# Attention and two gated layers on one core: a home for the sums of squares, chunk two's start and the last statistics planned with the next part, layer 2's decoding spaced

## The chip, the cores and the metric

The kernel runs on one core of one Trainium2 chip. A core has a matrix engine (TensorE, PE in the profile, with weight loads shown apart as PEld), a vector engine (DVE), an activation engine (ACT), a general engine (GpSimd, POOL) and a synchronising engine (SP) that here issues the transfers. The metric is the device time of one execution in microseconds, lower is better. Times of the trace are counted from the first instruction of its span.

## The reference, cut to what matters

```python
def reference(q, k, v, moe, moe2):            # q, k, v: 4 batches, 8 heads, 576 tokens, 64
    scores = where(mask, q @ k.T / 8, -1e9)   # heads 0-3: the last 32 positions,
    a = softmax(scores) @ v                   # heads 4-7: every 32nd position
    x = a.transpose(0, 2, 1, 3).reshape(2304, 512)
    xn = x / sqrt(mean(x * x) + 1e-6) * rms_g
    y = (silu(xn @ w_gate) * (xn @ w_val)) @ w_out         # 512 -> 1536 -> 512
    h = y @ w_in2                                          # 512 -> 2048
    return softplus(h) @ w_out2                            # 2048 -> 512
```

## The kernel before, in words

Each fp32 product is made of three products of halves: a number is split into a high part and the rest, both stored in a reduced matmul type, and `mm3` multiplies high by high, low by high and high by low. So `ob` (normalised tokens), `win` and `wout` (weights), `gh`/`gl` (gated values) and `tb` all come in pairs: ACT makes the high part (L257, L313, L333, L724) and DVE or POOL subtracts it for the rest (L262 on DVE, L264 on POOL). The tokens are cut into chunks at `CUTS` 0, 512, 1024, 1536, 2048, 2304. Chunks 0 and 1 are **side one**, computed plainly; chunks 2 to 4 are **side two**, where sums of chunks (`combine`, `build`, tile `tb`) and of weights let seven products stand for eight (`quad`).

Weights arrive as 64-bit words. `decode` turns one 128x512 block into fp32: a transfer into `raw` (512 KB, L277), one ACT instruction (L278), three DVE instructions (L279, L281, L284), and a transfer of the result to `w_kept` in DRAM (L287), from where later passes fetch it. A step f of layer 1 has three such blocks (`prep1`: two for `win`, one for `wout`); side two decodes layer 2's blocks ahead of time (`early2`).

The order of every engine's instructions comes from a planner. `pr.add` records work for an engine with an estimated duration; each `pr.emit()` closes a **part**, in which the planner lays out the recorded work by these estimates. Work in `side = True` is a second PE stream that is fitted in between the first. On each engine a part's instructions all come after those of the part before. The parts that matter here:

- Part 1: attention of batches 0 and 1 (`attend`, tiles without a tag). Each output block is squared and added up by POOL into `ssq`, the **sums of squares of side one** (128x1024). In the gaps stand the statistics of chunk 0 (`stats(0)`: a PE product of `ssq` with ones L356, ACT's Ln L358 and Exp L359, three DVE instructions L360, L362, L363, then `norm`, which multiplies the tokens `xs` by the result), `direct(0)` (the split into `ob`), and the `half` products of layer 1's steps f=0 and 1. At the end the same for chunk 1 (`stats(1)`, `direct(1)`) and the first two `chain1` (silu L735, product L736, split).
- Part 2: `side_a(f)` for f = 0 to 9 (f below `DEALT`), mixed with the attention of batches 2 and 3, whose tiles have the tag b (`klb0`, `qlb0`, `ksb0`, `qsb0` hold keys and queries; the first are loaded at L425 and L427 and completed with fixed patterns by DVE L390 and POOL L394). At its end stand the statistics of chunks 3 and 4, the **last turn**.
- Part 3: `side_a(10)`, `side_a(11)`, then `combine` and `build` of side two, its layer 1 (12 steps with a `quad` each), then layer 2 over both sides with `prep2` for its weights. `out1` (L769) and `out2` (L787) add finished products to `xs`.

The pool `at` of part 1 also holds `ssq`; part 2's pool `at2` reuses the same memory for the b tiles.

Of the kernel before, what the change touches and what calls it, by code (L numbers as in the profile page):

```python
# [27 lines left out]
CH = 512  # L28
# [8 lines left out]
DEALT = 10  # L37
LT, LT2, LV, EB = 4, 4, 5, 5
WARM = 9
EXTRA = {"gv": 2, "gh": 3, "gl": 3}  # L40
START = 14
HOLD = (12, 14)
# [122 lines left out]
def attn_glu_softplus(  # L165
# [36 lines left out]
    class Ring:  # L202
        def __init__(self, tiles, name, first=0):
            self.t, self.name, self.first, self.k = tiles, name, first, -1

        def next(self):
            self.k += 1
            i = self.k % len(self.t)
            return self.t[i], (f"{self.name}{self.first + i}", 0, 1 << 20)

    tb, ssq = [], []

    def sview(lo, hi):
        return ssq[0][:, lo:hi] if hi <= TA else ssq_b[:, lo - TA:hi - TA]
# [11 lines left out]
    xs = const.tile([128, KD * NT], F32, name="xs")  # L226
    ssq_b = const.tile([128, TB], F32, name="ssq_b")
# [146 lines left out]
    def attention(at, tag, bs, nq2, nv, npt, nsq, s_banks, t_banks, v_banks):  # L374
# [10 lines left out]
        def fixed(i):  # L385
            def spread(eng, t, key, h, x0, n, w, c0):
                dst = t[64:128, h, x0:x0 + n * w].rearrange("p (n w) -> p n w", w=w)
# [216 lines left out]
    def steps(at, after, ring_):  # L604
# [29 lines left out]
        return out + [None, (turn, (), (3, 4))]  # L634
# [203 lines left out]
    def prep2(p, all4):  # L838
        i = ((W1N + p) % 2, 0)
        o = 3 * W1N + 4 * p  # L840
        prep_in(i, [(o, None), (o + 2, None)], True, all4, "DVE")
# [4 lines left out]
    with tc.manual_schedule():  # L846
# [25 lines left out]
        at_step(16, prepare, 0, (0, 1), HOLD[0])  # L872
        at_step(17, prepare, 1, (0,), HOLD[1])
        at_step(START, stats, 0, f_banks)
        at_step(START, direct, 0)
        for f, r_ in ((0, f_banks), (1, s_banks)):
            for row in (0, 1):
                at_step(18 + f, half, f, row, r_)
# [13 lines left out]
        with ExitStack() as c2:  # L892
            at = c2.enter_context(tc.tile_pool(name="at", bufs=1))
            ssq.append(at.tile([128, TA], F32, name="ssq"))
            attend(attention(at, "", (0, 1), 2, 3, 4, 2, s_banks, t_banks, v_banks), fill)
            stats(1, t_banks)
            direct(1)
            table("silu_and_others")
            for f in (0, 1):
                g[f, 0] = chain1(gates[f, 0], gates[f, 1])  # L900
# [3 lines left out]
        for key, dt in (("gv", F32), ("gh", F32R), ("gl", F32R)):  # L904
# [7 lines left out]
        def side_a(f, queue):  # L912

            if f:
# [14 lines left out]
        with ExitStack() as c2:  # L929
# [3 lines left out]
            x.fixed(0)  # L933
            queue = steps(x, {1: (2,)}, tv)
# [3 lines left out]
            step(queue, len(queue))  # L938
            pr.emit(start=0)
        o_banks.t = banks.t[4:6] + banks.t[2:4]  # L940
        wc = ctx.enter_context(tc.tile_pool(name="wc", bufs=1))
# [4 lines left out]
        for f in range(DEALT, W1N):  # L946
            side_a(f, [])
# [3 lines left out]
        o_banks.t = banks.t[4:]  # L951
        build(*SIDES[1], False)
        for f in range(W1N):
# [16 lines left out]
            early2(2 * f)  # L970
# [98 lines left out]
```

## Time and profile before

| what | value |
|---|---|
| median of 3 runs | 977.6 us (975.78 to 978.59) |
| the profiled execution, its own time | 977.51 us |
| its span, first to last instruction | 975.7 us |
| mean granted TensorE clock | 0.963 |
| PE busy | 908.3 us (93%) |
| DVE busy | 723.5 us (74%) |
| ACT busy | 489.0 us (50%) |
| POOL busy | 213.2 us (22%) |
| moved by DMA | 103.12 MB, 35.3% of the engines' span |

The profiled execution lies within the runs, 0.1 us under the median. Its time is 1.8 us longer than its span, which is what lies around the first and last instruction. PE is busy nearly throughout; a share is an average over parts with different limits, so the parts have to be looked at singly.

### The profile page before, as it was taken

How to read it: one execution, taken by the hardware profiler on the slowest of the kernel's cores; microseconds unless marked ns; L12 is line 12 of the kernel's file. 1: busy time of each engine (PE TensorE's matmuls, PEld its weight loads, DVE VectorE, ACT ScalarE, POOL GpSimd, SP SyncE). 2: the span in 40 equal slices, each digit the busy share in tenths (PEclk: the TensorE clock that was granted, in tenths of full speed). 3: DMA queues.
4: the chain of work that ended last, by engine and by line, in shares of the span. 5: the costliest groups of instructions: out<-in, count | busy, mean ns of one | idle time of the engine just before them, and what ended most of it. 6: DMA issues, size and time to landing. Idle time of an engine off the chain costs nothing.

```text
span 975.7 us, 14001 instructions
## 1 busy us (share of the span) xinstructions
PE 908.3 (93%) x5244; PEld 746.2 (76%) x5244; DVE 723.5 (74%) x1198; ACT 489.0 (50%) x917; POOL 213.2 (22%) x187
## 2 busy tenths in 40 slices
PE   6877799999959899999999997999998999999998
PEld 5755678777837678888888876888886888888886
DVE  7696768897359888597887888787779736666654
ACT  5565566555254546545354545744455464434431
POOL 2453102141144543243233353000004000000000
PEclk8777899999988999999999999999999999999999
DMA  9834766744005245233433403431110411111002
GB/s 205 197 123 119 214 208 181 229 127 150 1 23 179 85 136 184 75 125 120 135 109 98 154 9 108 162 104 59 54 57 20 152 44 44 25 41 44 22 1 108
DMA packets 42036, 103.12 MB, mean 106 GB/s; under 512 B 5040, under 2 KB 5744, under 8 KB 41968
## 3 DMA queue, kind: packets, MB, share of 16 engines
q1 hardware_dynamic: 41968, 102.23, 35.3%
q8 instruction: 41, 0.67, 0.3%
q14 instruction: 27, 0.22, 0.1%
HBM read 79.66 MB, written 22.54 MB: 105 GB/s over the span
## 4 chain that ended last, share of the span: by engine, by line
PE 77%; DVE 15%; issue 3%; ACT 3%; DMA 2%; POOL 0%; SPq 0%; DVEq 0%; ACTq 0%; POOLq 0%
PE bank L342 71%; PE bank L449 3%; DVE xs L262 2%; PE bank L530 2%; DVE w L262 2%; PE bank L506 1%; DVE xs L769 1%; DVE cvu L281 1%; DVE win L262 1%; DVE cvu L279 1%; DVE ob L262 1%; DVE tb L262 1%; DMA ql<-q_t 1%; DVE gvx L262 1%; DVE gv L688 1%
## 5 line engine op out<-in xcount | busy, mean ns | idle before, releaser
L342 PE MATMUL bank<-ob,win 128*128 128x512 f32 (+1 forms) x1560 | 343.6, 367 | 26.0 <-ACT win L313 11.4
L342 PEld LDWEIGHTS bank<-ob,win 128*128 128x128 f32 x1560 | 270.0, 193 | 78.4 <-ACT win L313 11.8
L342 PE MATMUL bank<-tb,win 128*128 128x512 f32 x672 | 172.7, 392 | 7.8 <-ACT gvx L684 3.6
L342 PEld LDWEIGHTS bank<-tb,win 128*128 128x128 f32 x672 | 124.1, 188 | 37.1 <-ACT gv L684 5.0
L787 DVE TENSOR_TENSOR xs<-bank,xs 128x512 f32<-128x512 f32 x126 | 86.7, 689 | 49.1 <-PE bank L342 48.6
L313 ACT ACTIVATE win<-w 128x512 fp32r<-128x512 f32 (+1 forms) x136 | 83.2, 615 | 77.8 <-DVE w L262 34.6
L262 DVE TENSOR_TENSOR win<-w,win 128x512 fp32r<-128x512 f32 x112 | 80.0, 715 | 22.3 <-ACT win L313 22.0
L342 PE MATMUL bank<-wout,ghx 128*128 128x512 f32 x304 | 94.0, 391 | 0.6 <-DVE xs L787 0.5
L342 PE MATMUL bank<-ghx,wout 128*128 128x512 f32 x224 | 86.0, 403 | 0.5 <-ACT ghx L724 0.5
L342 PE MATMUL bank<-gh,wout 128*128 128x512 f32 (+1 forms) x256 | 83.1, 362 | 3.0 <-DVE xs L769 2.9
L342 PE MATMUL bank<-wout,gh 128*128 128x512 f32 x272 | 84.0, 390 | 0.0
L769 DVE TENSOR_TENSOR xs<-bank,xs 128x512 f32<-128x512 f32 (+1 forms) x100 | 62.8, 631 | 24.9 <-PE bank L342 24.3
L262 DVE TENSOR_TENSOR w<-w 128x256 f32<-128x256 f32 x112 | 65.9, 588 | 1.3
L342 PEld LDWEIGHTS bank<-wout,ghx 128*128 128x128 f32 x304 | 56.6, 188 | 13.2 <-DVE xs L787 1.8
L342 PE MATMUL bank<-wout,glx 128*128 128x512 f32 x152 | 59.3, 390 | 0.3 <-DVE glx L262 0.3
L342 PEld LDWEIGHTS bank<-wout,gh 128*128 128x128 f32 x272 | 50.8, 188 | 10.8 <-DVE xs L787 0.4
L281 DVE SCALAR_TENSOR_TENSOR cvu<-raw,cvu 128x512 uint32<-128x512 uint32 x68 | 56.6, 833 | 1.3
L342 PEld LDWEIGHTS bank<-gh,wout 128*128 128x128 f32 x256 | 46.9, 194 | 11.4 <-DVE xs L769 4.3
L342 PE MATMUL bank<-wout,gl 128*128 128x512 f32 x136 | 52.9, 389 | 0.0
L342 PEld LDWEIGHTS bank<-ghx,wout 128*128 128x128 f32 x224 | 43.1, 192 | 10.3 <-ACT ghx L724 0.9
L688 DVE TENSOR_TENSOR gv<-bank,gv 128x512 f32<-128x512 f32 x48 | 33.0, 687 | 20.5 <-ACT gv L684 14.1
L342 PE MATMUL bank<-gl,wout 128*128 128x512 f32 (+1 forms) x128 | 46.2, 361 | 1.7 <-POOL gl L264 1.7
(157 smaller groups left out, 1357.5 us busy)
## 6 DMA issues: line engine op xcount, KB each, us to landing
raw<-w SPq DMA_DIRECT2D x68, 512.0 KB, 4.0
w<-w_kept SPq DMA_DIRECT2D x56, 256.0 KB, 2.7
w_kept<-w SPq DMA_DIRECT2D x24, 256.0 KB, 3.4
w_kept<-cvt SPq DMA_DIRECT2D x22, 256.0 KB, 2.9
w_kept<-cvtx SPq DMA_DIRECT2D x22, 256.0 KB, 3.3
cvt<-w_kept SPq DMA_DIRECT2D x22, 256.0 KB, 2.7
cvtx<-w_kept SPq DMA_DIRECT2D x22, 256.0 KB, 2.8
out<-xs SPq DMA_DIRECT2D x18, 256.0 KB, 2.0
```

Of the source, the lines that this page charges most:

```text
L262: dve(n, lambda: getattr(nc.vector, name)(o, x, y), r, w)
L279: dve(512, lambda: nc.vector.tensor_scalar(out=u, in0=t.bitcast(U32), scalar1=0x80000000, scalar2=None, op0=ALU.bitwise_and), [kt], [ku], ...
L281: dve(512, lambda: nc.vector.scalar_tensor_tensor(out=u, in0=wlo, scalar=29, in1=u, op0=ALU.logical_shift_right, op1=ALU.bitwise_or), [kra ...
L313: act(n, lambda: nc.scalar.activation(h, t, AF.Copy), [kt], [reg(0, o + lo, o + hi)])
L342: lambda a=a, b=b, i=i, st=st, mv=mv: nc.tensor.matmul(o, lhsT=st[a], rhs=mv[b], start=(first and i == 0), stop=(last and i == m - 1), ski ...
L449: pr.add("PE", 108 if loc else 81, lambda a=a, h=h: nc.tensor.matmul(sp[64 * h:64 * h + 64, a * nk:(a + 1) * nk], lhsT=qt[:, h, q0 + a * s ...
L506: pr.add("PE", 109, lambda a=a, a0=a0, tp=tp: nc.tensor.transpose(tp[:kp, a * 128:a * 128 + 128], pv[:, a0 + a, :], id_sb), [kpv, all_of(" ...
L530: pr.add("PE", 81, lambda a=a, h=h, o=o, t=t: nc.tensor.matmul(xb[64 * h:64 * h + 64, a * nq:(a + 1) * nq], lhsT=vt[r0:r1, v0 + a, 64 * h: ...
L688: dve(CH, lambda: nc.vector.tensor_add(o[0], y[0], o[0]), [y[1], o[1]], [o[1]])
L769: dve(n, lambda: nc.vector.tensor_add(x, pb, x), [kp, kx], [kx])
L787: dve(DM, lambda: nc.vector.tensor_add(x, pb, x), [kp, kx], [kx])
```

## The change

Seven edits, in the order of the program:

1. `ssq` gets a tile of its own that stays. In part 2, once chunk 1's statistics are recorded, its two halves become two more buffers of the ring `gv`, in place of the two extra ones (`gvx0`, `gvx1`) that were allocated.
2. `stats(0)`, `direct(0)` and f=0's halves are recorded after `attend` as side work of part 1, not at a fixed step within it; `stats(1)`, `direct(1)`, f=1's halves and the first two `chain1` are recorded in part 2, so that they are planned together with it. The first weights are prepared from step 11, not 16.
3. The four larger fixed patterns of the b tiles (`klb0`, `qlb0`, two copies each) are written by POOL instead of DVE.
4. The last turn moves from the end of part 2 into part 3, after two empty places in step 10's queue; f=10's weights (three decodings) move into the end of part 2.
5. The banks 2 and 3 get correct keys in the output ring.
6. Layer 2's blocks 0 to 23 are decoded three for each f from 2 to 9, not two for each f from 0 to 11.
7. In layer 2, the two subtractions for the summed weights of `prep2` go to POOL for p=0 of both sides and p=1 to 3 of the first: ten instructions.

```diff
-EXTRA = {"gv": 2, "gh": 3, "gl": 3}
-START = 14
-HOLD = (12, 14)
+EXTRA = {"gh": 3, "gl": 3}
+HOLD = (8, 14)
...
+            self.keys = {}
...
-            return self.t[i], (f"{self.name}{self.first + i}", 0, 1 << 20)
+            return self.t[i], self.keys.get(i, (f"{self.name}{self.first + i}", 0, 1 << 20))
...
+    ssq = const.tile([128, TA], F32, name="ssq")
...
-        def fixed(i):
+        def fixed(i, swap={}):
             def spread(eng, t, key, h, x0, n, w, c0):
+                eng = swap.get(eng, eng)
...
-        return out + [None, (turn, (), (3, 4))]
+        return out, lambda: turn((), (3, 4))
...
-        prep_in(i, [(o, None), (o + 2, None)], True, all4, "DVE")
+        prep_in(i, [(o, None), (o + 2, None)], True, all4, eng)
...
-        at_step(16, prepare, 0, (0, 1), HOLD[0])
+        at_step(HOLD[0] + 3, prepare, 0, (0, 1), HOLD[0])
         at_step(17, prepare, 1, (0,), HOLD[1])
-        at_step(START, stats, 0, f_banks)
-        at_step(START, direct, 0)
-        for f, r_ in ((0, f_banks), (1, s_banks)):
-            for row in (0, 1):
-                at_step(18 + f, half, f, row, r_)
...
-            stats(1, t_banks)
-            direct(1)
-            table("silu_and_others")
-            for f in (0, 1):
-                g[f, 0] = chain1(gates[f, 0], gates[f, 1])
+            pr.side = True
+            stats(0, f_banks)
+            direct(0)
+            for row in (0, 1):
+                half(0, row, f_banks)
+            pr.side = False
             pr.emit()
...
-            if f:
+            if f and f != DEALT:
...
-            x.fixed(0)
-            queue = steps(x, {1: (2,)}, tv)
+            pr.side = True
+            stats(1, t_banks)
+            direct(1)
+            pr.side = False
+            for i in (0, 1):
+                fk["gv"].keys[len(fk["gv"].t)] = ("ssq", i * CH, i * CH + CH)
+                fk["gv"].t.append(ssq[:, i * CH:i * CH + CH])
+            for row in (0, 1):
+                half(1, row, s_banks)
+            table("silu_and_others")
+            for f in (0, 1):
+                g[f, 0] = chain1(gates[f, 0], gates[f, 1])
+            x.fixed(0, {"DVE": "POOL"})
+            queue, last_turn = steps(x, {1: (2,)}, tv)
...
             step(queue, len(queue))
+            prep1(DEALT, 0)
             pr.emit(start=0)
...
+        o_banks.keys = {i: (f"bank{i}", 0, 1 << 20) for i in (2, 3)}
...
-            side_a(f, [])
+            side_a(f, [None, None, (last_turn,)] if f == DEALT else [])
...
-            early2(2 * f)
-            early2(2 * f + 1)
+            for k in range(max(0, 3 * f - 6), min(3 * f - 3, 2 * W1N)):
+                early2(k)
...
-                i = prep2(p, c4 is not None)
+                i = prep2(p, c4 is not None, "POOL" if p == 0 or side == 0 and p < 4 else "DVE")
```

What stands in a row on an engine, before and after, at three places. The first is PE around the statistics of chunk 1, at the end of the first attention: `ssq` with ones is their product, `ob,win` are halves of layer 1, `klb0,qlb0` opens the second attention. First the kernel before, then the changed one:

```order
L530 MATMUL bank5_75<-pt3_118,vb1_106 64x54 x4
L342 MATMUL bank0_70<-ob_66,win0_89 128x512 x7
L342 MATMUL bank1_71<-ob_66,win0_89 128x512 x2
L356 MATMUL bank2_72<-ssq_96,ones_61 128x512
L342 MATMUL bank1_71<-ob_66,win0_89 128x512 x10
L342 MATMUL bank7_77<-ob_66,win0_89 128x512 x12
L449 MATMUL bank0_70<-klb0_928,qlb0_926 64x96 x10
```

```order
L532 MATMUL bank5_76<-pt3_118,vb1_106 64x54 x4
L343 MATMUL bank7_78<-ob_67,win0_90 128x512 x3
L343 MATMUL bank6_77<-ob_67,win0_90 128x512 x12
L357 MATMUL bank2_73<-ssq_65,ones_61 128x512
L343 MATMUL bank0_71<-ob_67,win0_90 128x512 x12
L343 MATMUL bank1_72<-ob_67,win0_90 128x512 x12
L343 MATMUL bank7_78<-ob_67,win0_90 128x512 x12
L451 MATMUL bank0_71<-klb0_875,qlb0_873 64x96 x10
```

Behind the statistics' product stood ten matmuls that do not need its result; now 24 do (banks 0 and 1, f=1 of chunk 0), and the block on bank 7 that needs chunk 1 comes after them.

The second place is SP's queue at the first load of part 2, with the semaphores that each transfer waits for; the kernel before, then the changed one:

```order
L287 DMA w_kept<-w32_82 128x512 [waits DMAHW6_49,DVE_49]
L427 DMA klb0_928<-k_loc 64x1728 [waits PE_49,DVE_49,Activation_49,Pool_49]
L425 DMA qlb0_926<-q_t 64x1216 [waits DMAHW0_49]
L277 DMA raw1_79<-w1 128x512 [waits DMAHW1_49]
L425 DMA qsb0_927<-q_t 64x1216 [waits DMAHW2_49]
```

```order
L288 DMA w_kept<-w32_83 128x512 [waits DVE_49]
L429 DMA klb0_875<-k_loc 64x1728 [waits DMAHW0_49,DMAHW7_49,PE_49,Pool_49]
L427 DMA qlb0_873<-q_t 64x1216
L278 DMA raw1_80<-w1 128x512 [waits DMAHW1_49]
L429 DMA ksb0_876<-k_str 64x1188 [waits DMAHW3_49]
```

The load of `klb0` no longer waits for DVE and ACT, which are the engines of chunk 1's statistics; the load of weights behind it stands in the same queue.

The third place is PE where the second attention ends and the statistics of chunks 3 and 4 stand (`ssq_b` with ones); the kernel before, then the changed one:

```order
L342 MATMUL bank6_76<-ob_66,win0_89 128x512 x12
L356 MATMUL bank3_73<-ssq_b_65,ones_61 128x512
L356 MATMUL bank2_72<-ssq_b_65,ones_61 128x256
L342 MATMUL bank7_77<-ob_66,win0_89 128x512 x12
L342 MATMUL bank4_74<-gh1_86,wout0_90 128x512
```

```order
L343 MATMUL bank5_76<-glx1_867,wout1_860 128x512
L343 MATMUL bank5_76<-ghx1_864,wout1_860 128x512
L357 MATMUL bank3_74<-ssq_b_66,ones_61 128x512
L357 MATMUL bank2_73<-ssq_b_66,ones_61 128x256
L343 MATMUL bank7_78<-ob_67,win0_90 128x512 x12
```

Two halves of step 10 and twelve output matmuls have moved ahead of the two statistics products. On DVE, the three decodings that stand behind the statistics before (f=10's) stand in part 2 now, and those of f=11 come ahead of them.

## Rows read from the trace of the kernel before

**Rows 1.** The page, busy time of each engine.

```profile
PE 908.3 (93%) x5244; PEld 746.2 (76%) x5244; DVE 723.5 (74%) x1198; ACT 489.0 (50%) x917; POOL 213.2 (22%) x187
```

**Rows 2.** Busy time in stretches: PE, PEld, DVE, ACT, POOL; clock, DMA share, GB/s.

```profile
76.60:92.20 15.60, 9.30 (x24) 5.95 (x25) 12.68 (x17) 10.36 (x17) 6.17 (x7) 0.69 0.34 88
92.20:123.30 31.10, 24.92 (x178) 19.50 (x178) 21.02 (x46) 15.48 (x26) 4.31 (x4) 0.88 0.83 223
123.30:275.50 152.20, 151.14 (x1124) 120.78 (x1123) 110.17 (x196) 78.30 (x147) 27.75 (x26) 1.00 0.48 141
349.60:560.00 210.40, 208.40 (x1082) 177.47 (x1083) 166.25 (x258) 106.05 (x194) 71.29 (x55) 1.00 0.40 127
...
282.40:349.50 67.10, 51.33 (x198) 40.11 (x198) 61.51 (x84) 30.08 (x53) 35.77 (x27) 0.85 0.37 118
...
292.50:349.60 57.10, 51.33 (x199) 40.11 (x199) 51.72 (x74) 25.95 (x47) 28.55 (x22) 0.90 0.41 129
```

**Rows 3.** PE from the first attention to the second: start, duration, idle before and releaser.

```profile
83.40 0.80 PE L342 MATMUL bank<-ob,win 128*128 128x512 f32 x1 [3.31 <-ACT ob L257]
86.82 5.06 PE L342 MATMUL bank<-ob,win 128*128 128x512 f32 x11 [2.63 <-DVE ob L262]
...
103.92 0.79 PE L449 MATMUL bank<-ksb,qsb 128*64 128x54 f32 x20 [2.27 <-DVE ebb L462]
...
111.01 5.49 PE L342 MATMUL bank<-ob,win 128*128 128x512 f32 x12 [3.34 <-ACT gv L735]
```

**Rows 4.** DVE in the same stretch.

```profile
68.05 0.24 DVE L480 RECIPROCAL mz<-mz 128x6 f32<-128x6 f32 x2
...
73.57 0.69 DVE L262 TENSOR_TENSOR win<-w,win 128x512 fp32r<-128x512 f32 x1 [1.33 <-ACT win L313]
79.34 0.69 DVE L360 SCALAR_TENSOR_TENSOR gv<-bank,ssq 128x512 f32<-128x512 f32 x1 [5.08 <-ACT ssq L359]
...
82.00 3.56 DVE L262 TENSOR_TENSOR xs<-xs,ssq 128x512 f32<-128x512 f32 x4
...
90.71 1.40 DVE L390 COPY qlb<-pat 64x576 f32<-64x576 f32 x2
```

**Rows 5.** SP's issue of the first load of part 2.

```profile
85.66 0.47 SPq L427 DMA_DIRECT2D klb<-k_loc  x1
```

**Rows 6.** ACT behind the first weights of part 2.

```profile
94.12 0.66 ACT L278 ACTIVATE cvtx<-raw 128x512 f32<-128x512 f32 x1 [4.46 <-DMA raw<-w]
```

**Rows 7.** PE from the end of the second attention to side two.

```profile
279.55 1.56 PE L356 MATMUL bank<-ssq_b,ones 128*128 128x512 f32 x4 [0.78 <-POOL ssq_b L570]
292.50 1.22 PE L342 MATMUL bank<-ob,win 128*128 128x512 f32 x2 [11.39 <-ACT win L313]
...
349.59 1.66 PE L342 MATMUL bank<-tb,win 128*128 128x512 f32 x6 [0.70 <-DVE xs L769]
```

**Rows 8.** DVE in the same stretch: a wait, one stretched instruction, two unhindered ones.

```profile
282.48 0.69 DVE L360 SCALAR_TENSOR_TENSOR gvx<-bank,ssq_b 128x512 f32<-128x512 f32 x1 [1.52 <-ACT ssq_b L359]
...
288.37 1.74 DVE L262 TENSOR_TENSOR gvx<-xs 128x512 f32<-128x512 f32 x1
...
308.99 0.41 DVE L279 TENSOR_SCALAR cvu<-w 128x512 uint32<-128x512 uint32 x1
309.32 0.68 DVE L262 TENSOR_TENSOR win<-w,win 128x512 fp32r<-128x512 f32 x1
```

**Rows 9.** POOL in the same stretch: the norm of chunks 2 to 4 begins.

```profile
285.18 10.31 POOL L264 TENSOR_TENSOR xs<-xs,ssq_b 128x512 f32<-128x512 f32 x8 [5.68 <-DVE ssq_b L363]
```

**Rows 10.** POOL by form, whole span: mean ns of one, then idle before.

```profile
L264 POOL TENSOR_TENSOR win<-w,win 128x512 fp32r<-128x512 f32 x24 | 33.6, 1402 | 35.5 <-ACT win L313 20.1 <-issue 14.3 <-PE bank L342 1.1
```

**Rows 11.** PE at the start of layer 2, its two longest waits.

```profile
573.92 0.80 PE L342 MATMUL bank<-gl,wout 128*128 128x512 f32 x1 [1.73 <-POOL gl L264]
...
599.46 1.66 PE L342 MATMUL bank<-tb,win 128*128 128x512 f32 x6 [2.28 <-ACT gvx L684]
```

More of the change, by code (lines that the diff above doesn't have):

```diff
@@ L208, in next @@
             i = self.k % len(self.t)
-            return self.t[i], (f"{self.name}{self.first + i}", 0, 1 << 20)
-    tb, ssq = [], []
+            return self.t[i], self.keys.get(i, (f"{self.name}{self.first + i}", 0, 1 << 20))
+    tb = []
     def sview(lo, hi):
-        return ssq[0][:, lo:hi] if hi <= TA else ssq_b[:, lo - TA:hi - TA]
+        return ssq[:, lo:hi] if hi <= TA else ssq_b[:, lo - TA:hi - TA]
     def ring(pool_, name, n, shape, dt=F32):
@@ L836, in early2, with prep2 @@
         decode(w2[k // 2, :, k % 2 * 512:(k % 2 + 1) * 512], t, kt, 3 * W1N + k)
-    def prep2(p, all4):
+    def prep2(p, all4, eng):
         i = ((W1N + p) % 2, 0)
         o = 3 * W1N + 4 * p
-        prep_in(i, [(o, None), (o + 2, None)], True, all4, "DVE")
+        prep_in(i, [(o, None), (o + 2, None)], True, all4, eng)
         for j in (0, 1):
@@ L893, in attn_glu_softplus @@
             at = c2.enter_context(tc.tile_pool(name="at", bufs=1))
-            ssq.append(at.tile([128, TA], F32, name="ssq"))
             attend(attention(at, "", (0, 1), 2, 3, 4, 2, s_banks, t_banks, v_banks), fill)
-            stats(1, t_banks)
-            direct(1)
-            table("silu_and_others")
-            for f in (0, 1):
-                g[f, 0] = chain1(gates[f, 0], gates[f, 1])
+            pr.side = True
[4 more added lines that the diff above has]
+            pr.side = False
             pr.emit()
@@ L903, in attn_glu_softplus @@
         wout += [wb.tile([128, 2, 512], F32R, name=f"wout{i}") for i in (1, 2, 3)]
-        for key, dt in (("gv", F32), ("gh", F32R), ("gl", F32R)):
+        for key, dt in (("gh", F32R), ("gl", F32R)):
             for i in range(EXTRA[key]):
@@ L950, in attn_glu_softplus @@
         drain(len(todo))
-        o_banks.t = banks.t[4:]
+        o_banks.t, o_banks.keys = banks.t[4:], {}
         build(*SIDES[1], False)
```

## The prediction, made before the changed kernel ran

> **What bounds the kernel now.** I read the page first. PE is busy for 93% of the span [rows 1], so only the other 67 us can be won without taking matmuls away, and no edit does that. Next, busy time by stretches. From 123 to 275 us PE works 151.1 of 152.2 us at clock 1.00, and from 350 to 560 us 208.4 of 210.4 [rows 2]: there PE is the bound. Two stretches are different. From 76.6 to 123.3 us, around chunk 1's statistics, PE works 9.30 of 15.6 and 24.92 of 31.1 us at clocks 0.69 and 0.88. From 292.5 to 349.6 us PE works 51.33 of 57.1 us, and just before it stood for 11.39 us [rows 2, 7]. I call these the seam and the hinge. Last I read the timelines of the engines in these two, for what each idle time waits for.
>
> At the seam, PE stops for the split of chunk 1 (3.31 and 2.63 us, released by ACT's and DVE's `ob`) and later for the second attention and for `gv` (2.27 and 3.34 us) [rows 3]. Behind the first two stands DVE: from the last reciprocal of the attention (68.05) to the first instruction of the statistics (79.34) it has nothing but decoding, and waits 1.33 and 5.08 us [rows 4]. Behind the later ones stand transfers. SP issues `klb0`'s load only at 85.66 [rows 5], since it waits for `ssq`'s readers, and the weights queued behind it reach ACT at 94.12 after a wait of 4.46 us [rows 6].
>
> At the hinge, the statistics of chunks 3 and 4 run at 279.55, and the next matmul waits until 292.50 for weights of step 10 [rows 7], which DVE decodes only behind those statistics [rows 8] and with POOL busy beside it. From 282.4 to 349.5 DVE works 61.51 of 67.1 us [rows 2]: it, not PE, sets the time until the first `tb` product at 349.59, which waits for a DVE eviction [rows 7].
>
> **The change, part by part.** The sum is made against the profiled execution (977.51 us, span 975.7), which is 0.1 us under the median, so no correction is made.
>
> *Seam, statistics.* Chunk 0's part no longer cuts into the attention at a fixed place; the planner puts its DVE work into the attention's tail. The tail from 68.05 to 79.34 is 11.3 us long and DVE is idle in 6.4 of it (1.33 + 5.08) [rows 4]. Work of chunk 0 that stood ahead of the tail fills most of it. I keep 1.6 us of idle: a gain of 4.8 us. Bounds: 0, if the attention's own chain (scores, exponent, reciprocal) decides when the tail begins, and 6.4.
>
> *Seam, cover.* Behind the product with ones stand 24 matmuls instead of 10. 14 more at 0.46 us each (12 in 5.49 at the low clock [rows 3]) are 6.4 us, about the two waits of 3.31 and 2.63 us; but they are work that was done earlier before, in other gaps of the attention, so only that part counts which no other gap would take. I take 1.7 us. Bounds 0 and 6.4. The pattern copies that leave DVE (`qlb0`'s pair took 1.40 us [rows 4], `klb0`'s about as much) are done by POOL, and DVE's four products with `xs` stretch to 3.56 us for four whenever POOL runs [rows 4]; these two cancel.
>
> *Seam, loads.* `klb0` no longer waits for the statistics. What it still waits for is POOL and PE of the attention, which end near 71 us; so SP's queue moves forward by up to 14 us from 85.66 [rows 5], and the weights with it. ACT's wait of 4.46 us [rows 6] goes, and with it most of PE's 2.27 and 3.34 us [rows 3], together 5.6: I take 4.0. Bounds 0 (PE waits then for DVE, which is busy for 21.02 of 31.1 us [rows 2]) and 5.6.
>
> Seam together: −10.5 us, bounds 0 and −18 (6.4 + 6.4 + 5.6); I hold −6 to −13 for likely.
>
> *Hinge.* f=10's three decodings go to part 2, where DVE works 110.17 of 152.2 us [rows 2]; a decoding is 1.5 us there (a first instruction 0.33 from start to start, then two of 0.60 [rows 8]), so the cover of 42 us is large. If it were not there they would cost the same as now. The wait of 11.39 us goes, but PE is not the bound of the stretch. DVE is: from 282.4 to 349.5 it has 84 instructions [rows 2]; 65 at 0.60 us, 8 of the short kind and 11 half-width ones at 0.33, are 45.4 us. It idles 5.6 us (67.1 less 61.51). The remaining 16.1 us are stretch while POOL works (0.68 becomes 1.74 [rows 8]): 0.45 us for each of POOL's 35.77 us [rows 2]. The change takes away three decodings (4.6 us), their three subtractions (1.8 us) and one layer 2 decoding (1.5 us). It begins about 1.4 us earlier, since the wait of 1.52 us for the exponent [rows 8] is filled with f=11's decoding. What is left is 37.5 + 5.6 + 16.1 = 59.2 us from 281.0, that is 340.2 instead of 349.6: −9.4 us. Bounds: −5 if the stretch grows with the decodings of f=11 that now meet POOL's products, and −24 if DVE keeps up (rival one).
>
> *Spaced decoding.* For f=2 to 9 of side two DVE gets one decoding more for each f, 1.5 us on some 17.5 (210.4/12). It works 166.25 of 210.4 us [rows 2], so it goes from 79% to 88%, and PE stays ahead: 0. If the cover fails in places, PE waits about 0.5 us for each of eight steps: +4.
>
> *Layer 2.* Ten subtractions go to POOL. PE's longest waits at that start are 1.73 us (for POOL's `gl`) and 2.28 us (for ACT's `gvx`) [rows 11]; neither is for DVE's `win`. DVE gets 1.3 us less for each p (two of 0.68 [rows 8], 0.60 in a row), where POOL takes 1.40 us for one [rows 10]. −1.5 us, bounds 0 and −5.
>
> *Keys, ring.* The two halves of `ssq` replace two buffers of the same size: 0.
>
> Sum: −10.5 − 9.4 − 1.5 = −21.4, so 977.5 − 21.4 = **956.1 us**, called 956.
>
> On the ten subtractions and four copies that move to POOL, the Trainium skill speaks against the change: SBUF — State Buffer, section "Who interferes with whom", says that the port pair which DVE and GpSimd share is an exclusive lock, and Perfetto Trace Analysis, section "Optimizing Scalar/DVE Operations", that moving work between these two might not help. The trace bears the first out, with 1.74 us beside 0.68 [rows 8].
>
> **The rivals.**
>
> *One: PE is the bound of the hinge.* If DVE no longer stands behind every eviction, the stretch is PE's own: 57.1 us from 292.50 to 349.6, less its idle 5.8 us and less some 5.7 us that its clock (0.90) costs [rows 2], is 45.6, from the end of step 9's products at 278.8 (279.55 less 0.78 [rows 7]): side two starts at about 325 (278.8 + 45.6). That is −24 instead of −9.4: 942 us. For it: DVE's share of POOL's stretch falls when f=10's work is gone. Against it: evictions are still interleaved with 37.5 us of DVE work and the same POOL work.
>
> *Two: the seam gives nothing, or little.* If the attention's tail is as long as its own chain, and the statistics of chunk 0 hold up PE's queue there (PE runs in order, so all the halves behind L356 wait for POOL's sums), the seam gives 0 to −3: 956 + 9 = 965 us. For it: PE's waits move easily from one engine to the next here, as its four waits have four releasers [rows 3]. Against it: 6.4 us of DVE's idle time lie there plainly [rows 4].
>
> *Three, the other side: the statistics of chunks 3 and 4 are late.* In the changed order 36 matmuls and f=11's decodings stand ahead of them. 36 matmuls are 16 us at the low clock (12 in 5.49 us [rows 3]) and 8 at the high one, which is twice it, so that the norm, which began at 285.18 [rows 9], begins at 292 to 301. From the norm's begin to the first `tb` product it was 64.4 us (349.59 − 285.18) [rows 7, 9]. If all of that is one chain, the kernel is slower once the norm starts after 349.6 + 12 − 64.4 = 297.2 (12 being what the seam and layer 2 give). At 299 it would be 979 to 980 us. Against it: that stretch was filled by DVE's queue, not by the norm's 10.31 us [rows 9], and 7.9 us of that queue are gone.
>
> *Four: POOL's help costs what it saves.* Each of the ten subtractions that DVE sheds saves it 0.60 us, but stretches one of its others by 1.06 (1.74 − 0.68 [rows 8]); with ten it is +4.6 us instead of −1.5: 962 us. By the mean stretch (0.45 for each of POOL's us, 1.40 us for one [rows 10]) it is 0.63 against 0.60, that is nothing. The two pages named above stand behind this rival.
>
> That the change does not do what it says is not a rival of its own: its three places can be read in the order of instructions.
>
> **How the numbers follow.** A measurement here cannot tell less than about 0.3%, 3 us, from no change. The forecast (949 to 961) has 0.49, rival one 0.14, rival two 0.18, rival four 0.08, and rival three 0.09, of which 0.06 end slower by over 0.3% and 0.03 within it. The other 0.02 are slack, one each for no change and for slower by a cause I don't see. Faster: 0.49 + 0.14 + 0.18 + 0.08 = 0.89; same 0.03 + 0.01; slower 0.06 + 0.01. The range of 8 in 10 reaches down to rival one and up beyond rival two: 941 to 969.
>
> **What would show it.** At the seam: `klb0` issued near 72 us, no DVE wait of 5 us before L360, PE's four waits under 4 us together. At the hinge: no PE wait of over 3 us between 270 and 300 us of the old time, DVE still busy for over 85% from the statistics to the first `tb` product, and this product some 20 us earlier than 349.6 (10.5 + 9.4). In layer 1 of side two: 210 us as before. The prediction is wrong if the first `tb` product comes later than about 340, if PE waits for POOL's norm or for `tb` there, or if side two takes over 214 us.

## The result, and the profile after

The changed kernel took 961.86 us (median of 4 runs, 961.42 to 963.24), the kernel before 976.83 us on the same chip (4 runs, 975.78 to 978.59): ratio 0.9847, interval 0.9828 to 0.9867, so 15.0 us or 1.5% faster. The profiled execution took 961.84 us, its span is 959.9 us. The forecast was 956 us, with a range of 941 to 969.

The forecast was 6 us too low, but no single term did that: the first third of the program gained more than I said, and the rest gave some of it back. To see it, I compare when the same instruction begins on DVE in two traces. Instructions on DVE keep their number by kind (100 evictions of `out1`, 84 additions of the quads, 126 evictions of `out2`), so the n-th of a kind is the same work. The table has the start in the kernel before minus the start in each kernel: how far it is ahead, in us. The experiments are named in the next section.

| kernel | first `out1` (160.7 before) | first quad (353.3) | last quad of layer 1 (571.2) | fourth of layer 2 (609.1) | second side (767.1) |
|---|---|---|---|---|---|
| changed | 12.7 | 25.1 | 21.7 | 16.7 | 15.8 |
| changed, again | 13.1 | 25.5 | 21.4 | 16.4 | 15.6 |
| e1 spacing undone | 12.3 | 24.3 | 24.5 | 22.0 | 20.1 |
| e2 subtractions undone | 11.5 | 24.0 | 20.1 | 17.5 | 17.3 |
| e3 both undone | 13.2 | 25.1 | 25.3 | 22.5 | 22.5 |
| e8 seam alone | 13.5 | 17.5 | 18.1 | 15.3 | 15.2 |
| e6 weights early only | 12.2 | 22.9 | 23.0 | 23.5 | 23.5 |
| e7 statistics late only | 14.2 | 16.4 | 15.0 | 15.5 | 15.5 |
| e9 home alone | 7.6 | 8.8 | 8.8 | 7.7 | 7.7 |
| e12 chunk 1 in part 1 | 4.2 | 7.8 | 8.3 | 5.6 | 5.5 |
| e4 patterns on DVE | 11.3 | 22.9 | 23.0 | 21.8 | 21.8 |
| e10 subtractions p=1 to 3 | 13.3 | 25.2 | 26.1 | 21.0 | 21.8 |
| e11 subtractions p=0 | 14.5 | 26.5 | 26.6 | 23.8 | 22.2 |

One trace stands for each kernel. Ten of these kernels (all but e9, e12 and e4) have the same seam, yet lie between 11.5 and 14.5 us in the first column; the spread is there already when PE comes to the product of chunk 1's `ssq` with ones (68.16 to 70.96 us). So a lead over the kernel before is known to about 1.5 us. Differences between two columns repeat to some tenths of a microsecond.

So the changed kernel is 12.7 us ahead at the end of the seam (10.5 forecast) and wins another 12.4 us up to the first quad, at the hinge (9.4 forecast); then it loses 3.4 us in side two's layer 1 (0 forecast) and 5.9 us in layer 2 (a gain of 1.5 forecast).

Line numbers of the changed kernel are a few higher: L357 is the product with ones, L361 the first DVE instruction of the statistics, L429 the load of keys, L771 the eviction. Busy time by stretches, the seam's two, the hinge's and side two's layer 1 (columns as in [rows 2]; the second and the fourth end where the same number of matmuls is done as in the kernel before, 178 and 1082):

```profile
69.60:88.70 19.10, 12.69 (x41) 7.61 (x40) 16.14 (x23) 12.91 (x21) 7.41 (x11) 0.91 0.69 196
88.70:111.38 22.68, 21.81 (x178) 17.31 (x177) 20.41 (x41) 14.31 (x24) 6.80 (x6) 1.00 0.77 222
...
278.10:323.60 45.50, 37.52 (x154) 28.99 (x152) 44.89 (x56) 20.43 (x38) 35.97 (x26) 0.96 0.21 64
323.60:538.10 214.50, 209.86 (x1082) 178.60 (x1083) 173.11 (x259) 106.92 (x196) 71.49 (x57) 0.99 0.41 128
```

From 88.7 us PE is now busy for 21.81 of 22.7 us at clock 1.00, where it was 24.92 of 31.1 at 0.88 [rows 2]. At the hinge DVE is busy for 44.89 of 45.5 us with 56 instructions instead of 84 in 67.1 us [rows 2]: it is still the bound there. Side two's layer 1 takes 214.5 us for the work that took 210.4 [rows 2]. PE's timeline of the changed kernel at the same places (start, duration, then idle before and releaser):

```profile
69.67 1.13 PE L357 MATMUL bank<-ssq,ones 128*128 128x512 f32 x2
72.68 3.29 PE L343 MATMUL bank<-ob,win 128*128 128x512 f32 x12 [1.89 <-ACT win L314]
77.42 3.30 PE L343 MATMUL bank<-ob,win 128*128 128x512 f32 x12 [1.44 <-ACT win L314]
83.31 0.50 PE L343 MATMUL bank<-ob,win 128*128 128x512 f32 x1 [2.60 <-ACT ob L258]
84.04 0.98 PE L343 MATMUL bank<-ob,win 128*128 128x512 f32 x3 [0.23 <-DVE ob L263]
...
88.69 1.05 PE L451 MATMUL bank<-klb,qlb 128*64 128x96 f32 x20
...
97.06 0.79 PE L451 MATMUL bank<-ksb,qsb 128*64 128x54 f32 x20
...
101.66 3.02 PE L343 MATMUL bank<-ob,win 128*128 128x512 f32 x12 [0.87 <-ACT gv L737]
...
274.36 1.45 PE L357 MATMUL bank<-ssq_b,ones 128*128 128x512 f32 x4
...
312.18 0.50 PE L343 MATMUL bank<-gh,wout 128*128 128x512 f32 x1 [3.75 <-DVE xs L771]
...
323.60 2.75 PE L343 MATMUL bank<-tb,win 128*128 128x512 f32 x6 [2.23 <-DVE xs L771]
...
579.17 2.39 PE L343 MATMUL bank<-tb,win 128*128 128x512 f32 x6 [3.17 <-ACT ssq L686]
```

Of the four waits at the seam [rows 3], 3.31 us became 2.60, and 2.63, 2.27 and 3.34 are down to 0.23, nothing and 0.87; two new ones, 1.89 and 1.44 us, are for the weights of f=1, whose 24 halves stand behind the product now. The wait of 11.39 us before the hinge [rows 7] is gone; the two longest that are left at the hinge are for DVE's evictions. The first `tb` product comes at 323.60, 26.0 us earlier. But the wait of 2.28 us in layer 2 [rows 11] has grown to 3.17.

### The profile page after: what moved, and what is told of

Read it like the earlier page. It is cut to its first block, busy times and chain, and to the rows that moved or that the text cites. A ratio compares the mean times of both kernels' runs of the same rounds, so it can differ in the third digit from the quotient of the medians.

```text
span 959.9 us, 14020 instructions
## 1 busy us (share of the span) xinstructions
PE 906.0 (94%) x5244; PEld 742.4 (77%) x5244; DVE 725.6 (76%) x1184; ACT 488.9 (51%) x917; POOL 229.8 (24%) x201
## 3 DMA queue, kind: packets, MB, share of 16 engines
q1 hardware_dynamic: 41968, 102.23, 35.9%
## 4 chain that ended last, share of the span: by engine, by line
PE 70%; DVE 19%; DMA 4%; issue 3%; ACT 3%; POOL 1%; SPq 0%; DVEq 0%; ACTq 0%
PE bank L343 65%; DVE w L263 3%; PE bank L451 2%; DVE xs L771 2%; DVE cvu L282 2%; PE bank L532 2%; DVE cvu L280 1%; PE bank L508 1%; DMA w<-w_kept 1%; DMA id_sb<-ident 1%; DVE xs L263 1%; DVE wout L263 1%; DVE win L263 1%; DVE tb L263 1%; DVE gv L690 1%
## 5 line engine op out<-in xcount | busy, mean ns | idle before, releaser
L343 PE MATMUL bank<-ob,win 128*128 128x512 f32 (+1 forms) x1560 | 336.9, 362 | 12.0 <-ACT ob L258 3.8
L343 PEld LDWEIGHTS bank<-ob,win 128*128 128x128 f32 x1560 | 265.2, 190 | 64.2 <-ACT win L314 4.6
L343 PE MATMUL bank<-tb,win 128*128 128x512 f32 x672 | 175.5, 397 | 12.0 <-ACT ssq L686 5.5
L263 DVE TENSOR_TENSOR win<-w,win 128x512 fp32r<-128x512 f32 x102 | 72.7, 714 | 29.1 <-ACT win L314 28.8
L265 POOL TENSOR_TENSOR win<-w,win 128x512 fp32r<-128x512 f32 x34 | 49.2, 1449 | 155.1 <-ACT win L314 143.5
L771 DVE TENSOR_TENSOR xs<-bank,xs 128x512 f32<-128x512 f32 (+1 forms) x100 | 62.2, 630 | 15.0 <-PE bank L343 14.2
L263 DVE TENSOR_TENSOR w<-w 128x256 f32<-128x256 f32 x112 | 71.9, 642 | 1.4
L343 PEld LDWEIGHTS bank<-wout,gh 128*128 128x128 f32 x272 | 50.9, 188 | 10.5
L282 DVE SCALAR_TENSOR_TENSOR cvu<-raw,cvu 128x512 uint32<-128x512 uint32 x68 | 51.7, 760 | 1.4
L265 POOL TENSOR_TENSOR gl<-ssq,gh 128x256 fp32r<-128x256 f32 (+1 forms) x21 | 22.3, 1064 | 120.1 <-ACT gh L726 120.1
L726 ACT ACTIVATE gh<-ssq 128x512 fp32r<-128x512 f32 (+1 forms) x41 | 23.0, 564 | 54.2 <-PE bank L343 37.1
```

Source lines behind the costliest of these rows:

```text
L263: dve(n, lambda: getattr(nc.vector, name)(o, x, y), r, w)
L265: pool(n, lambda: getattr(nc.gpsimd, name)(o, x, y), r, w)
L282: dve(512, lambda: nc.vector.scalar_tensor_tensor(out=u, in0=wlo, scalar=29, in1=u, op0=ALU.logical_shift_right, op1=ALU.bitwise_or), [kra ...
L343: lambda a=a, b=b, i=i, st=st, mv=mv: nc.tensor.matmul(o, lhsT=st[a], rhs=mv[b], start=(first and i == 0), stop=(last and i == m - 1), ski ...
L726: act(n, lambda: nc.scalar.activation(h, src, AF.Copy), [ksrc], [kh])
L771: dve(n, lambda: nc.vector.tensor_add(x, pb, x), [kp, kx], [kx])
```

## The experiments

Each kernel is the changed one with the edit shown, if nothing else is said; kernels sent together ran on one chip beside the kernel before.

**The two late edits, undone one at a time and together.** Beside them the changed kernel again (label r, no edit).

```diff
e1: -            for k in range(max(0, 3 * f - 6), min(3 * f - 3, 2 * W1N)):
    -                early2(k)
    +            early2(2 * f)
    +            early2(2 * f + 1)
e2: -                i = prep2(p, ..., "POOL" if p == 0 or side == 0 and p < 4 else "DVE")
    +                i = prep2(p, ..., "DVE")
e3: both
```

> The changed kernel with layer 2's decodings put back to two for each f from 0 to 11; all else as changed. Theory of the prediction (the spacing costs nothing, since PE bounds side two's layer 1): within 1 us of the changed kernel, about 962 us, and the loss of the lead there (26.0 us ahead at the first tb product, 22 at the end of layer 1) remains. Rival (the third decoding for each f makes DVE late for the quads' evictions): 958 to 959 us, the lead at the end of layer 1 is 25 to 26 us.

> The changed kernel with the ten subtractions of layer 2's summed weights back on DVE. Theory of the prediction (they give 1.5 us on POOL): 963 to 964 us. Rival (POOL's help costs more than it saves; the wait of 3.17 us at 579 us, after which TensorE's granted clock is 0.69 for 10 us, comes from POOL holding up DVE or being late itself): 957 to 959 us, the wait back to about 2.3 us, the clock 1.00 behind it.

> The changed kernel with both edits undone, layer 2's spacing and the ten subtractions. Theory of the prediction: 963 to 964 us. Rival, both losses are real and add up: 953 to 956 us. If only one of them is real it lies where that one alone lies.

> The changed kernel as it is, on the same chip as the three runs that undo an edit, as their measure: 961 to 963 us by either theory; the same wait of about 3 us and the same low clock near 579 us if these belong to the kernel and not to one execution.

Measured, with 977.67 us for the kernel before: changed 960.85 us (ratio 0.9830, 0.9802 to 0.9857), e1 956.96 (0.9791, 0.9766 to 0.9816), e2 957.52 (0.9782, 0.9753 to 0.9812), e3 954.09 (0.9755, 0.9727 to 0.9782). Each edit costs 3 to 4 us and they add up: 3.9 and 3.3 against 6.8. My theory fell for both. The rivals' times are met by e2 and e3; e1 is 1 us better than its rival said. One part of e2's rival is not met: the wait went back to 2.27 us, but the granted clock fell behind it all the same (last section). In the second trace of the changed kernel the wait is 3.17 us again and the clock low behind it, so they do not belong to one execution. e3 is faster than both kernels of the case.

Where e1's part lies shows in PE's waits of the changed kernel in layer 1 of side two, and in the busy time of 40 us at about the same place, first of the changed kernel, then of e1 (16 matmuls more):

```profile
470.48 1.67 PE L343 MATMUL bank<-tb,win 128*128 128x512 f32 x6 [1.19 <-DVE gv L690]
478.62 1.66 PE L343 MATMUL bank<-tb,win 128*128 128x512 f32 x6 [0.91 <-ACT gv L686]
506.82 0.39 PE L343 MATMUL bank<-gh,wout 128*128 128x256 f32 x1 [1.00 <-DVE ssq L738]
```

```profile
440.00:480.00 40.00, 37.73 (x192) 31.59 (x191) 35.39 (x56) 18.22 (x33) 11.86 (x10) 1.00 0.46 150
```

```profile
438.00:478.00 40.00, 39.33 (x208) 33.68 (x208) 31.82 (x50) 18.34 (x34) 13.20 (x10) 1.00 0.38 120
```

DVE is busy for 35.39 instead of 31.82 of 40 us, 88% against 80%, and PE stands 2.3 instead of 0.7 us. Over the steps f=2 to 9 DVE's share goes from 84% in e1 to 88%, and PE's idle time from 0.8 to 4.1 us. What the wait at 470.48 was for is a quad's addition (L690, at 469.75) behind a decoding's first DVE instruction (L280), for which DVE itself had waited 1.49 us. The wait at 478.62 came another way, which these three instructions of the changed kernel show:

```profile
473.60 1.52 DVE L263 TENSOR_TENSOR w<-w 128x256 f32<-128x256 f32 x1
475.04 1.78 DVE L285 SCALAR_TENSOR_TENSOR cvtx<-cvtx,cvu 128x512 uint32<-128x512 uint32 x1
476.74 0.68 DVE L690 TENSOR_TENSOR ssq<-bank,ssq 128x512 f32<-128x512 f32 x1
```

A half-width and a full-width instruction take 1.52 and 1.78 us while POOL works (instead of 0.41 and 0.69). ACT has waited 2.98 us when the addition behind them is done at 477.42; it then does silu (L737) and the copy (L686) that PE waits for at 478.62.

**The seam.** e8 undoes the two late edits and the hinge too, so that of the larger edits only the seam is left (the keys of edit 5 stay in it; no run takes them away alone, and none takes the earlier start of the first weights away alone); e9 is the kernel before with nothing but the first edit; e12 is e8 with chunk 1's chain closed into part 1.

```diff
e8: e3, and
    -            if f and f != DEALT:
    +            if f:
    -            prep1(DEALT, 0)
    +            last_turn()
                 pr.emit(start=0)
    -            side_a(f, [None, None, (last_turn,)] if f == DEALT else [])
    +            side_a(f, [])
e9: the kernel before, and
    +    ssq.append(const.tile([128, TA], F32, name="ssq"))
    -            ssq.append(at.tile([128, TA], F32, name="ssq"))
         and the ring's two buffers from its halves, in part 2
e12: e8, and in part 1, ahead of its pr.emit()
    +            stats(1, t_banks)
    +            direct(1)
    +            for row in (0, 1):
    +                half(1, row, s_banks)
    +            table("silu_and_others")
    +            for f in (0, 1):
    +                g[f, 0] = chain1(gates[f, 0], gates[f, 1])
     (not in part 2)
```

> Of the change only the seam is left: the sums of squares' own home with the two buffers from it, the new order around chunk 1's statistics, and the patterns on POOL. The last statistics and step 10's weights, the spacing and the ten subtractions are as before. The prediction's seam term says 10.5 us under the kernel before, 966 to 968 us; the trace of the changed kernel, 12.4 us ahead at the end of the second attention, says 964 to 966 us and the old wait of 11 us behind the statistics. Rival two of the prediction (the seam gives little): 974 to 977 us.

> The kernel before with the first edit alone: the sums of squares in a tile of their own, their halves as two buffers of the ring in part 2. The prediction's term for the loads (4.0 of the seam's 10.5 us) says 973 to 974 us, the first load of part 2 issued about 75 us instead of 85.7, and no ACT wait of 4.5 us for the weights. Rival (the loads are not what the second attention waits for, since DVE is behind with chunk 1 anyway): 976 to 978 us, though the load is issued early.

> The seam alone (961 us), but chunk 1's statistics, split, f=1's halves and the first two gated products closed into part 1, so that they are not planned together with the second attention; in PE's order no matmul is left between the statistics' product and the halves that need its result. The prediction's term for the cover (1.7 us) says 963 us. If planning the two parts together is what made the seam worth 16.6 us and not 10.5: 966 to 969 us, which is where the home alone lies.

Measured: e8 961.1 us (before 977.73; ratio 0.9830, 0.9810 to 0.9849), e9 969.44 us on the same chip (0.9912, 0.9895 to 0.9930), e12 971.57 us (before 977.41; 0.9936, 0.9914 to 0.9958; one of its six runs took 3123.76 us and is left out). The seam is worth 16.6 us, more than its expectation from the trace, and rival two (974 to 977) fell; the home alone 8.3 us, twice its term. Closing chunk 1 into part 1 costs e8 10.5 us. That is more than either expectation said (963, or 966 to 969): e12 ends at or above the home alone, with intervals that overlap. So planning the two parts together is worth more than the 1.7 us that I gave to cover. The lines that decide are e9's issue of the keys and its busy time over the second attention's start, where before had 24.92 of 31.1 us [rows 2, 5]:

```profile
77.02 0.47 SPq L429 DMA_DIRECT2D klb<-k_loc  x1
```

```profile
91.90:115.60 23.70, 22.18 (x178) 17.57 (x177) 21.33 (x47) 14.78 (x25) 4.77 (x4) 0.99 0.76 212
```

The same 178 matmuls are over in 23.7 instead of 31.1 us: PE's idle time there falls from 6.2 to 1.5 us, and its busy time from 24.92 to 22.18 us, because the clock granted is 0.99 and not 0.88. I had priced only the first part. In e12, PE's line at the statistics:

```profile
80.77 1.02 PE L357 MATMUL bank<-ssq,ones 128*128 128x512 f32 x2
87.42 0.80 PE L343 MATMUL bank<-ob,win 128*128 128x512 f32 x1 [5.63 <-ACT ob L258]
90.84 4.26 PE L343 MATMUL bank<-ob,win 128*128 128x512 f32 x11 [2.63 <-DVE ob L263]
```

The product with ones stands behind f=1's halves and comes at 80.77 instead of 69.67, although POOL's last sum for it was done at 72.07, so that it stands 8.7 us in PE's row; and nothing is left to cover its 5.63 us. So the place of f=1's 24 matmuls, behind the product and not ahead of it, matters; e12 changes the place and the cover at once and does not say how much each is.

**The hinge, one move at a time**, both on top of e3.

```diff
e6: -            prep1(DEALT, 0)
    +            last_turn()
    +            prep1(DEALT, 0)
                 pr.emit(start=0)
    -            side_a(f, [None, None, (last_turn,)] if f == DEALT else [])
    +            side_a(f, [])
e7: -            if f and f != DEALT:
    +            if f:
    -            prep1(DEALT, 0)
                 pr.emit(start=0)
```

> The kernel with both late edits undone (954 us), and of the hinge's two moves only one: step 10's weights decoded in part 2, the last statistics where they were before. If the moved decodings carry the hinge's gain (DVE's queue is shorter, PE has its weights): 953 to 957 us, no wait of 11 us. If it is the later place of the statistics that carries it: 962 to 966 us.

> The other half: the last statistics in step 10's queue, step 10's weights decoded in part 3 as before. If the moved decodings carry the gain: 962 to 968 us, since PE waits some 10 us for step 10's weights, and the statistics stand behind it. If the later place of the statistics carries it: 953 to 957 us.

Measured beside e8 on one chip: e6 954.49 us (0.9763, 0.9741 to 0.9784), e7 962.49 us (0.9854, 0.9830 to 0.9879); e8 is at 961.1. The moved decodings carry the gain; the later statistics by themselves give nothing that the runs can tell, and with the decodings moved they give nothing either (e3 954.09). The reason can be read on DVE between the statistics and the first `tb` product, here in e6 and e7:

```profile
269.90:326.20 56.30, 48.55 (x195) 38.23 (x194) 55.47 (x71) 25.70 (x47) 37.41 (x27) 0.94 0.30 93
```

```profile
284.50:332.50 48.00, 36.98 (x153) 29.15 (x152) 47.98 (x59) 22.04 (x40) 37.08 (x26) 0.96 0.20 67
```

DVE is full in both. e7's stretch is shorter, but it begins 13.5 us later (the statistics' first DVE instruction is at 284.06, in e6 at 270.56). The work that moved out of it stands ahead of the statistics now, and so does PE's wait for step 10's weights, in e7:

```profile
269.49 5.83 PE L343 MATMUL bank<-ob,win 128*128 128x512 f32 x12 [4.69 <-ACT win L314]
```

After 4.69 us of waiting, these twelve matmuls take 5.83 us, at a granted clock of 0.50, where twelve take 3.02 us elsewhere (at 101.66 above).

**The subtractions, in two groups, and the patterns**, the first two on top of e1, the third on e3.

```diff
e10: -  ... "POOL" if p == 0 or side == 0 and p < 4 else "DVE"
     +  ... "POOL" if side == 0 and 0 < p < 4 else "DVE"
e11: +  ... "POOL" if p == 0 else "DVE"
e4:  -            x.fixed(0, {"DVE": "POOL"})
     +            x.fixed(0)
```

> The kernel with the spacing undone (957 us, with all ten subtractions on POOL; 954 us with none), with six of the ten on POOL: p=1 to 3 of the first side. If the cost sits at the start of each side's layer 2, where POOL is busy with sums for tb and the waits grew (3.17 us instead of 2.28, and 0.94, 1.67 and 1.49 us instead of 0.69 and 1.43): these six are free, 953 to 955 us. If each subtraction costs by itself (the prediction's rival four): 956 us.

> The other four of the ten: p=0 of both sides on POOL, the rest on DVE, spacing undone. If the cost sits at the start of each side: all of it is here, 956 to 958 us. If each subtraction costs by itself: 955 us.

> The kernel with spacing and subtractions undone (954 us), with the four larger patterns of the b tiles back on DVE. The prediction let them cancel (2.5 us off DVE against the stretch that POOL causes): 953 to 955 us. If they were part of the seam's surplus: 956 to 957 us, the second attention's first matmul 2 us later.

Measured, with 977.41 us for the kernel before: e10 956.9 us (0.9789, 0.9766 to 0.9813), e11 955.82 (0.9783, 0.9758 to 0.9808), e4 956.8 (0.9789, 0.9766 to 0.9811). The times do not tell e10 from e11, nor either from e1 and e3: inconclusive. The traces do, one place each. In e10 the wait at the first side's start is 3.19 us and the second side has its old waits; in e11 the first wait is 2.27 us and the second side has these:

```profile
709.76 1.66 PE L343 MATMUL bank<-tb,win 128*128 128x512 f32 x6 [0.94 <-ACT ssq L686]
713.07 1.66 PE L343 MATMUL bank<-tb,win 128*128 128x512 f32 x6 [1.65 <-ACT gv L686]
716.21 1.66 PE L343 MATMUL bank<-ob,win 128*128 128x512 f32 x6 [1.48 <-DVE gv L690]
```

So the first side's longer wait (0.9 us) belongs to p=1 to 3, and the second side's (1.6 us in the table, 23.8 to 22.2) to p=0: the cost is at the starts of both sides, as I expected, but not by the p that I had named. From the third column of the table to the last, e3 loses 2.8 us, e10 4.3 and e11 4.4: the six cost 1.5 us and the four 1.6.

The patterns on POOL can't be read from the first column (11.3 us in e4, just under the spread of the kernels that have them). Counted from chunk 1's product with ones to the first `out1`, e4 takes 79.8 us and the ten others 77.9 to 78.5, so they are worth 1.4 to 1.9 us there; in the times it is 2.7 us across two chips, with intervals that overlap. The second attention's first matmul is not 2 us later in e4 (88.98, others 86.80 to 89.87).

## Why the prediction was right, and where its steps were off

**The bound at the two places was right.** The seam and the hinge hold nearly all that was won, and the hinge was and stayed DVE's: rival one (PE the bound, 942 us) did not come, with DVE at 44.89 of 45.5 us. Rival two (the seam gives little) fell with e8. Rival three did not come either: the norm began at 280.7, and the `tb` product waits for an eviction, not for the norm; e7, where the statistics come latest, is no slower than 962.5.

**Seam, statistics and cover (4.8 and 1.7 forecast, together 3.5 measured).** The second attention's first product came at 88.69 instead of 92.22. The first half of the step held: with chunk 0's work planned into its gaps the first attention ends earlier. POOL's last sum of squares is done at 69.62 instead of 76.60, and PE's product with ones starts at 69.67 instead of 76.65, 7.0 us earlier (in e9, which has only the first edit, at 76.77). The step that failed is that this would bring the statistics forward: their first DVE instruction came only 0.3 us earlier. ACT's Ln stands in ACT's row behind the splits of two of f=1's weights, and each of these waits for DVE's decoding:

```profile
72.00 0.63 ACT L314 ACTIVATE win<-w 128x512 fp32r<-128x512 f32 x1 [2.47 <-DVE w L285]
...
76.73 0.63 ACT L314 ACTIVATE win<-w 128x512 fp32r<-128x512 f32 x1 [3.53 <-DVE w L285]
77.27 0.67 ACT L359 ACTIVATE ssq<-bank,eps 128x512 f32<-128x512 f32 x1
```

So Ln begins 6.5 us after its product was done (70.80). Nor did DVE's idle time in the tail shrink, which I had counted as the gain: the last reciprocal is at 59.08 now, and from there to the statistics DVE waits 6.5 us, where it was 6.4. Only the tail is longer, 20.0 instead of 11.3 us. Cover did not shorten PE's waits: behind the product they are 6.4 us (1.89, 1.44, 2.60, twice 0.23), where they were 5.9. The rest of the 3.5 us is won behind the statistics' start:

```profile
79.08 0.69 DVE L361 SCALAR_TENSOR_TENSOR gv<-bank,ssq 128x512 f32<-128x512 f32 x1 [0.99 <-ACT ssq L360]
...
81.26 1.89 DVE L263 TENSOR_TENSOR xs<-xs,ssq 128x512 f32<-128x512 f32 x3
83.29 0.69 DVE L263 TENSOR_TENSOR ob<-xs,ob 128x512 fp32r<-128x512 f32 x1
```

DVE's first part of the split is at 83.29, after three products with `xs`, where PE waited until 86.82 for it [rows 3].

**Seam, loads (4.0 forecast, 8.4 measured in the changed kernel, 7.4 in e9).** Mechanism right, size off by a factor of two. `klb0` was issued at 77.22, not near 72, because SP's queue holds the store of decoded weights until DVE is done at 76.7; even so the stretch shrank from 31.1 to 22.7 us for the same 178 matmuls. I had counted PE's idle time, and left out that its matmuls behind the waits ran at a lower granted clock. Seam together: 12.7 us in the trace against 10.5 (3.5, 8.4 and 0.8 behind the stretch), so two errors of opposite sign nearly cancelled, which is luck.

**Hinge (9.4 forecast; 12.4 in the stretch, 7.6 of it by the hinge's own edit).** The form of the sum was right, its count wrong. Per instruction 0.60 us (0.33 for half widths and first steps), plus idle, plus the stretch by POOL gives, for the stretch from the statistics to the first `tb` product:

| kernel | instructions | at full speed | idle | length | left for stretch | POOL busy |
|---|---|---|---|---|---|---|
| before | 84 | 45.3 | 5.5 | 67.1 | 16.3 | 35.9 |
| e8 | 78 | 42.8 | 2.5 | 62.5 | 17.2 | 35.9 |
| e6 | 71 | 38.3 | 0.2 | 55.7 | 17.2 | 37.4 |
| changed | 55 | 29.8 | 0.6 | 45.4 | 15.0 | 36.0 |

The stretch is 0.42 to 0.48 us for each of POOL's us in all four. I took out 15 instructions (7.9 us). The kernel took out 14 more (7.6 us), f=11's three decodings with two of their subtractions, and two evictions and a product of the gates, since the order puts them ahead of the statistics. I had written that f=11's decoding fills the wait ahead of them, and left it in the sum. Against it the statistics began later than I said: 278.2, where 281.0 less the seam's lead would have been near 268. And the edit alone is not worth 12.4: e8, without it, already wins 4.0 us there (13.5 to 17.5), with six instructions and 3 us of idle time less than before, which my term for the seam did not hold. The edit is the difference of e3 and e8, 25.1 less 17.5 in the trace and 7.0 us in the times.

**Spaced decoding (0 forecast, a loss of 3.4 in the trace and 3.9 in the times).** The failed step is "PE stays ahead". DVE's load went up nearly as worked out (88% over the eight steps), but that is a mean; single waits and POOL's stretch gather ahead of the quad's addition, as the two waits above show. The stated bound, +4, was the case, and so was one of the stated signs of being wrong: side two's layer 1 took 214.5 us, over 214.

**Layer 2 (a gain of 1.5 forecast; a loss of 5.9 in the trace, 3.1 of it by the subtractions, which lose 3.3 in the times).** Rival four was right in direction, with 3.1 us where it said 4.6: what POOL takes over stretches DVE just where the quad's addition is waited for. In the changed kernel two of the moved subtractions (568.31 and 572.36) stand ahead of POOL's four `ob` products, which so run until 577.94:

```profile
573.61 4.33 POOL L265 TENSOR_TENSOR ob<-xs,ob 128x256 fp32r<-128x256 f32 x4
```

```profile
575.01 1.23 DVE L282 SCALAR_TENSOR_TENSOR cvu<-raw,cvu 128x512 uint32<-128x512 uint32 x1
...
577.29 0.68 DVE L690 TENSOR_TENSOR gv<-bank,gv 128x512 f32<-128x512 f32 x1
```

The addition at 577.29 comes behind three instructions that take 1.23, 1.23 and 1.09 us meanwhile, and the wait of 3.17 us hangs on it, through ACT. What the Trainium skill says (SBUF — State Buffer, section "Who interferes with whom", an exclusive lock on the port pair of DVE and GpSimd; Perfetto Trace Analysis, section "Optimizing Scalar/DVE Operations", that such offloading might not help) agrees with these ten instructions: 1.23 us for L282 beside 0.69 without POOL (at 478.12), and a loss of 3.1 us. It does not hold for the four pattern copies, which stand where DVE was the one waited for and POOL was idle, and which gained 1.4 to 1.9 us by the trace, although the decodings beside them are stretched (in e4 the statistics begin 7.7 us after the start of their product, in the changed kernel 9.4).

**The sum.** The seam gained 2.2 us more than forecast and the hinge 3.0; the spacing took 3.4 and layer 2 took 7.4 that were not in the sum. Had the first two come as forecast, the kernel would have taken 967 us and not 962. That the time lies within 6 us of the forecast is so in part luck.

**What is left open.** At the start of layer 2 most of the faster kernels, e3 among them, lose another 2.6 to 2.8 us that is in no wait (table, fourth column against third: e3 25.3 to 22.5); the changed kernel's 5.9 are 3.1 by the subtractions and this. It is the granted clock, below; why it fell in these and not in the kernel before was not settled. The times of e3 and e6 (954.1 and 954.5) can't be told apart, though the trace of e6 has no such loss.

## What to carry to other kernels

Where one engine is the bound of a stretch, count its queue between two marks, instruction by instruction, in the order that the change really makes, and price the neighbour that stretches it by its busy time; here 0.45 us for each of POOL's microseconds gives the lengths of all four kernels in the table within 1.2 us. An idle engine ahead of a wait is not a gain yet: look which other engine's row the next step stands in, and behind what. Price a wait of the matrix engine with the matmuls behind it at their granted clock, not by its idle time alone. A mean load of 88% was no cover for work in which one late instruction is waited for: ask what stands in the queue just ahead of it.

## What the runs showed of the hardware that I had not expected

The matrix engine's granted clock falls in short stretches even after small waits, and not after all of the same size. Layer 2's start in the changed kernel, in e3 and in the kernel before (two rows each, in this order; columns as in [rows 2]):

```profile
575.00:581.00 6.00, 2.83 (x11) 1.88 (x9) 4.22 (x6) 2.15 (x4) 2.95 (x3) 0.90 0.55 168
581.00:587.00 6.00, 5.31 (x14) 3.75 (x13) 1.54 (x3) 3.44 (x7) 0.00 (x0) 0.53 0.17 44
```

```profile
569.00:575.00 6.00, 3.73 (x16) 2.81 (x15) 4.83 (x7) 2.67 (x7) 2.82 (x3) 0.98 0.55 156
575.00:581.00 6.00, 5.31 (x13) 3.63 (x13) 2.27 (x5) 2.51 (x6) 0.00 (x0) 0.50 0.45 152
```

```profile
594.00:600.00 6.00, 3.72 (x17) 2.77 (x16) 4.83 (x7) 2.67 (x7) 3.11 (x3) 1.00 0.50 161
600.00:606.00 6.00, 5.31 (x23) 4.05 (x22) 3.94 (x7) 4.41 (x9) 0.00 (x0) 1.00 0.53 165
```

In e3 and in the kernel before the waits are the same (2.27 and 2.28, then 0.69 us) and so is PE's busy time in the second stretch, 5.31 us; but before it does 23 matmuls at clock 1.00, and in e3 13 at 0.50, the lower of the two levels (1.2 GHz). That is the 2.8 us. Of the other traces with the same two waits (2.27 or 2.28 and 0.69 us), the clock fell in e2, e8, e11 and e12, which lose 2.6 to 2.8 us there, and for about half as long in e4 and e9, which lose 1.2 and 1.1. In e6 and e7 the first wait is 1.73 us; there it did not fall, and nothing was lost. The Trainium skill (TensorE: Matmul & The Clock Gate, section "Part 1: The HAM clock gate (the "warmup" mystery)") says that the block which sets the clock keeps its own time and not the kernel's. By that, the same waits may cost the clock in one kernel and not in the other; the rows agree, and no run here shows the mechanism.
